# Linear branch in blocks of four tiles, and a transpose of two-token words, in a gated mix of softmax and linear attention

## The chip, the cores and the metric

One core of a Trainium2 chip runs the whole kernel. The metric is the time of one execution in device microseconds; lower is better. The kernel before is given by three runs, and one further execution was taken with the hardware profiler; the profile shows what every engine did in that execution.

## The reference, cut to what matters

The input x has 2048 tokens of 512 features in bf16. Two attention branches of 32 heads with 16 features per head read the same x, and a gate per token mixes their outputs.

```python
x = A_x                                               # (1, 2048, 512) bf16
g = _sigmoid((x * gate_w).sum(-1, keepdims=True))
# branch A: softmax attention, 32 heads of 16
scores = jnp.einsum("bhqd,bhkd->bhqk", q, k) * (Dh ** -0.5)
a = jnp.einsum("bhqk,bhkd->bhqd", _softmax(scores), v)      # then reshaped, @ wo
# branch B: linear attention with learned feature maps
pq = jnp.einsum("bhsd,hdf->bhsf", q, w_phi);  pk likewise from k
phi_q = jnp.concatenate([_softmax(pq), _softmax(-pq)], axis=-1);  phi_k likewise
kv = jnp.einsum("bhsf,bhsd->bhfd", phi_k, v);  z = jnp.einsum("bhsf->bhf", phi_k)
o = (phi_q @ kv) / (phi_q @ z + 1e-6)                       # then reshaped, @ wo
return g * a + (1 - g) * b
```

## The kernel before, in words

The kernel first describes all its work as a list of operations with their data dependences, a priority (`prio`, a due time counted in packs, below) and a modelled cost. `Plan.order` then writes one fixed queue per engine: at each step it takes the operation that can start first by its own costs, and among those that are ready the one with the lowest priority value. The queues are emitted as they stand, with semaphore waits. On the chip each engine works through its queue strictly in order. So every change of a cost, a due time or a share in the code can move instructions on all queues.

**Branch A, the attention.** Queries are cut into 4 chunks of 512, keys into 16 tiles of 128. A *unit* is one head, one key tile and one query chunk: scores of 128 keys by 512 queries in one PSUM bank. Four units, of four heads, make a *pack*; there are 512 packs and 2048 units. A group of 16 packs (all key tiles for four heads) accumulates into one bank. For each unit TensorE computes the scores (L979), somebody computes the exponential, and TensorE multiplies the result by the values (L1099). Two engines compute exponentials:

- ScalarE (ACT) takes the units called *mine*, in groups of three and two banks by turns (`GROUPS = (3, 2)`), one instruction a group (L1030). The five banks form a ring: the scores of group k wait for the exponential of group k-2.
- VectorE (DVE) takes the units called *away*. `SHARES` has one number for each of the 32 groups: how many of its 64 units go to DVE. A batch is mostly five units (`NB = 5`; `FIRST` and `LAST` give the sizes of the first and last batches). For each unit the scores are copied as scaled integers into `vt` (L880); then five instructions over the whole batch compute the exponential through `vf` into `vu` (L902, L904, L905, L906, L890). `vt` has two halves, `vf` one, `vu` three slots. The linear branch uses the same `vt` and `vf` as work space.

`_norm` follows every group of 16 packs. `n_t1` (L1128) transposes the accumulated bank in blocks of 32x32 into `T1` in f32, so that tokens lie on partitions. After every second group, `n_den` (L1135), `n_rec` (L1137) and `n_mul` (L1139) divide by the sum of the exponentials and the gate, with the result in `T2` in bf16, and `n_back` (L1144) transposes `T2` back into `onTA`. The last two of the 32 groups are normalised one by one (`alone`), the last one in four blocks of 128 tokens. `_out_a` (L1455) and `_out_last` (L1483) multiply `onTA` by the output weights, with 128 tokens of `onTA` as the stationary operand that TensorE loads.

**Branch B, the linear attention.** It works on token tiles of 128, two at a time: `_b_pair` projects two tiles (L682, evacuated at L1241 into `bq`), computes the softmax feature maps with a chain of 22 (keys) or 23 (queries) DVE instructions in `_b_exp`, `_b_scale` and the tail of `_b_pair` (L1258 to L1324), and uses `btree` for the maxima and sums. There are 8 pairs for the keys and 8 for the queries. `_b_kv` accumulates keys times values for four tiles; `_b_phit` transposes the query features by DMA and `_b_num` forms numerator and denominator. `K0, SK, Q0, SQ` space the due times of these pieces.

**Queue of SyncE (SP).** It issues the loads and all DMA transposes. At the start the order is: loads of x, the weights of branch B's keys (`wb1`) and others; the DMA transposes of x for the token blocks 2 and 3 (`xT<-xn`, L605); two loads of attention weights; then the DMA transpose of branch B's key weights (`WT<-WB`, L1200), which `_b_fuse` multiplies by the feature weights (L1209) and copies back with DVE (L1214). `KREL` is the pack from which the planner may issue that transpose, `XREL` the one from which the remaining attention weights may be loaded, `VREL0` the one for the first value projection, `OREL` the release of the last output products.

Of the kernel before, what the change touches and what calls it, by code (L numbers as in the profile page):

```python
# [7 lines left out]
ALU = mybir.AluOpType  # L8
AX = mybir.AxisListType

P = 128
D = 512
H = 32
DH = 16
TOK = 128
QCH = 512
SCALE = float(DH) ** -0.5
F32, BF16 = dt.float32, dt.bfloat16
# [4 lines left out]
EVEN, ODD = 0.34370964, 0.07826797  # L23
# [344 lines left out]
class _Kernel:  # L368
# [8 lines left out]
    XREL, KD, VD = 4, 8, 1  # L377
    BYDMA = (2, 3)
    KREL = 7
    EARLY = 27  # L380
    VREL0 = 3
    FIRST = (3, 4)
    LAST = (4, 3)
    OREL = 2
# [30 lines left out]
    def _memory(self, ctx):  # L415
# [50 lines left out]
        self.bq = sb("bq", [P, 3, 2, 2 * D], BF16)  # L466
        self.btree = sb("btree", [P, 32, 8, 4], BF16)
        self.bsum = sb("bsum", [P, P], F32)
        self.brec = sb("brec", [P, P], FP16)
# [319 lines left out]
    def _gate(self):  # L789
# [32 lines left out]
        for j in range(4):  # L822
# [6 lines left out]
    SHARES = (0, 3, 0, 12, 0, 4, 0, 13, 10, 4, 8, 2, 12, 3, 5, 8,  # L829
              5, 10, 13, 13, 0, 7, 6, 3, 12, 10, 12, 5, 11, 8, 13, 9)  # L830
# [290 lines left out]
    def _norm(self, ch, b0, nb, side, last, dst, b_dst, due, job, alone=False):  # L1121

        op = self.plan.op
        b1 = b0 + nb
        T1, T2, rinv = self.T1[:, :, b0:b1], self.T2[:, b0:b1], self.rinv[:, :, b0:b1]
        b_T1, b_T2, b_rinv = self.b_T1, self.b_T2, self.b_rinv
        part = nb / 16
        op("DVE", lambda e: e.transpose(T1[:, side].rearrange("p b s -> p (b s)"), self._bank(job)[:, 0:32 * nb]),  # L1128
           0.09 + 0.542 * part, deps=last, writes=[b_T1[side]], name="n_t1", prio=due - self.TPRIO, release=job)
        if not (side or alone):  # L1130
            return
        lo, hi = (side, side + 1) if alone else (0, 2)
        n, reads = hi - lo, b_T1[lo:hi]
        den, h = T1[:, lo:hi, :, 16], self.gh[:, 0, ch, b0:b1][:, None, :].to_broadcast([P, n, nb])
        op("DVE", lambda e: e.tensor_tensor(rinv[:, lo:hi], den, h, ALU.mult), 0.09 + 0.014 * n, reads=reads + [self.b_g],  # L1135
           writes=[b_rinv], name="n_den", prio=due)
        op("DVE", lambda e: e.reciprocal(rinv[:, lo:hi], rinv[:, lo:hi]), 0.063 + 0.1 * n * part, reads=[b_rinv],  # L1137
           writes=[b_rinv], name="n_rec", prio=due)
        op("DVE", lambda e: e.tensor_tensor(  # L1139
            T2.rearrange("p b (s d) -> p s b d", s=2)[:, lo:hi], T1[:, lo:hi, :, 0:16],  # L1140
            rinv[:, lo:hi, :, None].to_broadcast([P, n, nb, 16]), ALU.mult), 0.08 + 0.258 * n * part,
           reads=reads + [b_rinv], writes=[b_T2], name="n_mul", prio=due)
        if side == 1:
            op("DVE", lambda e: e.transpose(dst[:, 32 * b0:32 * b1], T2.rearrange("p b s -> p (b s)")), 0.09 + 0.537 * part,  # L1144
               reads=[b_T2], writes=[b_dst], name="n_back", prio=due)

    K0, SK, Q0, SQ = 18.0, 8.25, 191.0, 15.25

    def _branch_b(self):
        op, NT, NQC = self.plan.op, self.NT, self.NQC  # L1150
        B = Buf
        self.b_bq = [B() for _ in range(3)]
        self.b_WT = B()
        self.b_WP = [B() for _ in range(2)]
        self.b_tree, self.b_bsum, self.b_brec = B(), B(), B()
# [7 lines left out]
        self.outs, self.held = [], []  # L1163
        self.n_pair = 0
# [6 lines left out]
        for t in range(0, NT, 2):  # L1171
            due = self.K0 + self.SK * t
            self.linear.append((due, lambda t=t, due=due: self._b_keys(t, due)))
        for t in range(0, NT, 2):
            due = self.Q0 + self.SQ * t
            self.linear.append((due, lambda t=t, due=due: self._b_queries(t, due)))

    def _b_keys(self, t, due):
        self._b_v(t, due)
        self._b_v(t + 1, due + 1)  # L1180
        slots = self.held + [self._b_pair(1, t, due)]
        if t % 4 == 0:
            self.held = slots
            return
        self.held = []
        self._b_kv(t - 2, slots, due + 12)
        if t == self.NT - 2:
            self._b_kvbd(self.Q0 - 2)

    def _b_queries(self, t, due):  # L1190
        phi = self._b_pair(0, t, due)
        self._b_phit(t, phi, due + 12)
        self._b_num(t, due + 20)
        if t % 4 == 2:
            for tt in range(4):
                self._b_out(tt)
# [31 lines left out]
    def _b_pair(self, s, t0, due):  # L1228
        op = self.plan.op
        slot = self.n_pair % 3  # L1230
        self.n_pair += 1
        b = self.b_bq[slot]
        bq = self.bq[:, slot]
        war, parts = list(b.readers), []
        for k in range(2):
# [10 lines left out]
        b.writers, b.readers = parts, []  # L1246
        x = bq.rearrange("p t (g f i) -> p (t g) f i", f=DH, i=4)
        tree = self.btree[:]
        half = self.btree[:].bitcast(FP16)
        last = lambda t: t.rearrange("p (g i) -> p g i", i=4)  # L1250
        two = lambda n: 0.057 + n * 0.000525
        spread = lambda t: t[:, :, None, :].to_broadcast([P, 32, DH, 4])

        def chain(ops, off, bufs):
            for name, cost, fn in ops:
                op("DVE", fn, cost, reads=bufs, writes=bufs, name=name, prio=due + off)
        self._b_exp(bq, spread(tree[:, :, 0]), b, due, two)
        chain([("b_sum", two(1024), lambda e: e.tensor_tensor(half, x[:, :, 0:8], x[:, :, 8:16], ALU.add))]  # L1258
              + [("b_sum", two(128 * n), lambda e, n=n: e.tensor_tensor(half[:, :, 0:n], half[:, :, 0:n],
                                                                       half[:, :, n:2 * n], ALU.add)) for n in (4, 2)]  # L1260
# [284 lines left out]
```

## Time and profile before

| | |
|---|---|
| median of 3 runs | 841.67 us (841.08 to 842.1) |
| the profiled execution | 841.6 us |
| its span, first to last instruction | 839.8 us |
| granted TensorE clock | 1.000 |
| busy: PE, DVE, ACT | 803.1, 805.9, 828.9 us |
| instructions: PE, DVE, ACT | 8734, 1119, 736 |

The span is 1.8 us shorter than the time of the same execution; that rest lies outside the first and the last instruction. Busy times count an engine as busy while at least one of its instructions is under way, so successive instructions that overlap are counted once. Part of PE's work is filler: L1108 multiplies by zeros (3076 instructions in the page), which adds nothing to the result.

### The profile page before, as it was taken

Reading aid. Unit: us, or ns where it says so; the run is one execution under the profiler, and the core shown is the slowest. Engines: PE = TensorE matmul, PEld = TensorE weight load, DVE = VectorE, ACT = ScalarE, POOL = GpSimd, SP = SyncE. Lnnn points to the kernel's source line nnn. Section 1 sums busy time; section 2 is a strip of 40 time slices with the busy share of each in tenths; the row PEclk is TensorE's granted clock in tenths of the full one; section 3 lists DMA queues with packets and bytes.
Section 4 is the critical chain, followed back from the end, with each engine's and each line's share of the span. In section 5 each row is a group of like instructions: output and inputs, shape, how many; then the busy total and the mean of one; then the engine's idle time right before and its main releaser. Section 6 shows DMA issues by size and latency. Waiting matters only on the chain.

```text
span 839.8 us, 19654 instructions
## 1 busy us (share of the span) xinstructions
PE 803.1 (96%) x8734; PEld 265.0 (32%) x8776; DVE 805.9 (96%) x1119; ACT 828.9 (99%) x736; POOL 7.9 (1%) x14
## 2 busy tenths in 40 slices
PE   9999999999999999999999999999999999999997
PEld 5323333333322232223323233223322322322334
DVE  4799999999999999999999999999999999999995
ACT  7999999999999999999999999999999999999997
POOL 3000000000000000000000000000000000000000
PEclk9999999999999999999999999999999999999999
DMA  9700000000000000011101101102101100100000
GB/s 216 193 2 7 2 2 7 2 7 2 8 1 2 8 2 7 2 24 23 28 18 27 32 15 27 20 13 51 33 14 33 26 21 2 39 7 2 2 2 27
DMA packets 49028, 20.02 MB, mean 24 GB/s; under 512 B 38704, under 2 KB 48944, under 8 KB 48944
## 3 DMA queue, kind: packets, MB, share of 16 engines
q1 hardware_dynamic: 48272, 18.58, 9.9%
q8 instruction: 68, 1.11, 0.6%
q10 hardware_dynamic: 672, 0.20, 0.1%
q14 instruction: 16, 0.13, 0.1%
HBM read 6.31 MB, written 2.10 MB: 10 GB/s over the span
## 4 chain that ended last, share of the span: by engine, by line
ACT 74%; DVE 22%; PE 3%; issue 0%
ACT ET L1030 74%; DVE vt L880 3%; DVE vu L890 2%; DVE vf L902 1%; DVE vu L906 1%; DVE vf L905 1%; DVE bq L1306 1%; DVE VB L1225 1%; DVE vt L1298 1%; PE ps L979 1%; DVE bq L1308 1%; DVE bq L1241 1%; DVE bq L1318 1%; DVE vu L904 1%; DVE btree L1294 1%; DVE V L784 1%
## 5 line engine op out<-in xcount | busy, mean ns | idle before, releaser
L1030 ACT ACTIVATE ET<-ps 128x1536 bf16<-128x1536 f32 x731 | 826.6, 1375 | 0.8 <-PE ps L979 0.7
L979 PE MATMUL ps<-qT,kT 32*128 32x512 bf16 (+2 forms) x2248 | 320.6, 364 | 26.2 <-ACT ET L1030 17.0
L1108 PE MATMUL ps<-kT,zero 128*32 128x512 bf16 (+1 forms) x3076 | 256.9, 384 | 0.3 <-DVE rinv L1137 0.3
L1099 PE MATMUL ps<-ET,V 128*32 128x512 bf16 (+2 forms) x2000 | 195.8, 364 | 0.6 <-ACT ET L1030 0.3
L979 PEld LDWEIGHTS ps<-qT,kT 32*128 32x128 bf16 x2248 | 84.3, 91 | 304.1 <-ACT ET L1030 213.3
L880 DVE TENSOR_SCALAR vt<-ps 128x512 uint32<-128x512 f32 x221 | 145.6, 684 | 4.0 <-PE ps L979 3.8
L890 DVE SCALAR_TENSOR_TENSOR vu<-vt,vu 128x2560 int16<-128x2560 uint32 (+3 forms) x46 | 124.7, 2710 | 0.2
L1108 PEld LDWEIGHTS ps<-kT,zero 128*32 128x32 bf16 x3076 | 68.2, 95 | 107.2 <-issue 82.0
L1099 PE MATMUL ps<-vu,V 128*32 128x512 bf16 (+1 forms) x248 | 80.9, 359 | 0.0
L1099 PEld LDWEIGHTS ps<-ET,V 128*32 128x32 bf16 x2000 | 54.5, 96 | 56.4 <-issue 32.0
L905 DVE TENSOR_TENSOR vf<-vf 128x2560 f16<-128x2560 f16 (+3 forms) x46 | 65.8, 1430 | 0.3
L906 DVE TENSOR_TENSOR vu<-vu,vf 128x2560 f16<-128x2560 f16 (+3 forms) x46 | 65.8, 1429 | 0.3
L902 DVE TENSOR_SCALAR vf<-vt 128x2560 f16<-128x2560 uint8 (+3 forms) x46 | 65.9, 1432 | 0.2
L682 PE MATMUL ps<-WB,xT 128*128 128x512 bf16 x166 | 48.3, 382 | 3.1 <-issue 1.8
L904 DVE TENSOR_SCALAR vu<-vf 128x2560 f16<-128x2560 f16 (+3 forms) x46 | 36.4, 792 | 0.3
L682 PE MATMUL ps<-xT,WA 128*128 128x512 bf16 (+1 forms) x124 | 35.6, 379 | 0.1
L1128 DVE STREAM_TRANSPOSE T<-ps 128x512 f32<-128x512 f32 (+1 forms) x35 | 23.2, 662 | 4.7 <-PE ps L1099 4.7
L1099 PEld LDWEIGHTS ps<-vu,V 128*32 128x32 bf16 x248 | 21.6, 96 | 19.2 <-issue 13.1
L1241 DVE TENSOR_SCALAR bq<-ps 128x512 bf16<-128x512 f32 x32 | 21.7, 679 | 1.6 <-PE ps L682 1.6
L682 PEld LDWEIGHTS ps<-WB,xT 128*128 128x128 bf16 x192 | 14.4, 97 | 27.0 <-issue 12.2
L1306 DVE TENSOR_TENSOR bq<-vt 128x1024 f16<-128x1024 f16 x32 | 21.7, 678 | 0.3
L1298 DVE TENSOR_TENSOR vt<-vt,btree 128x2048 bf16<-128x2048 bf16 x16 | 19.5, 1218 | 0.3
(96 smaller groups left out, 442.5 us busy)
## 6 DMA issues: line engine op xcount, KB each, us to landing
qT<-qraw SPq DMA_DIRECT2D x120, 16.0 KB, 1.8
xn<-in_A_x_dram SPq DMA_DIRECT2D x3, 512.0 KB, 7.0
WB<-in_B_wqkv_dram SPq DMA_DIRECT2D x3, 512.0 KB, 6.9
out_dram<-WB SPq DMA_DIRECT2D x12, 128.0 KB, 1.7
WA<-in_A_wqkv_dram SPq DMA_DIRECT2D x3, 384.0 KB, 4.5
xn<-in_A_x_dram SPq DMA_DIRECT2D x2, 256.0 KB, 3.7
WoA<-in_A_wo_dram SPq DMA_DIRECT2D x1, 512.0 KB, 4.3
WoB<-in_B_wo_dram SPq DMA_DIRECT2D x1, 512.0 KB, 5.1
```

The costliest lines, as they stand in the source:

```text
L682: mm = op("PE", lambda e, c=c: e.matmul(self._bank(job)[:, 0:n], lhs(c), rhs(c), start=(c == 0), stop=(c == 3)), self.c_pe(n), reads=reads ...
L880: parts.append(op("DVE", lambda e, j=j, job=job: e.tensor_scalar(vt[:, j, :], self._bank(job), SCALE * LOG2E * 2.0 ** 24, 2.0 ** 31, op0=A ...
L890: o = op("DVE", lambda e: e.scalar_tensor_tensor(out=flat(vu).bitcast(I16), in0=flat(vt), scalar=2.0 ** -17, in1=flat(vu), op0=ALU.mult, o ...
L902: ("_frac", two, lambda e: e.tensor_scalar(vf, frac, 1 / 256, ROOT, op0=ALU.mult, op1=ALU.add), [b_vt], [b_vf]),
L904: lambda e: e.tensor_scalar(vu, vf, CUBE, SQUARE, op0=ALU.mult, op1=ALU.add), [b_vf], [b_vu]),
L905: ("_sq", two, lambda e: e.tensor_tensor(vf, vf, vf, ALU.mult), [b_vf], [b_vf]),
L906: ("_cube", two, lambda e: e.tensor_tensor(vu, vu, vf, ALU.mult), [b_vf, b_vu], [b_vu]),
L979: ins = e.matmul(out[u][:, cols], self.kT[32 * i:32 * i + 32, cp, kt * TOK:(kt + 1) * TOK], self.qT[32 * i:32 * i + 32, s, q], start=True, ...
L1030: o = plan.op("ACT", lambda e: e.activation(self.ET[:, a % NS:a % NS + n, :], self.ps[:, a % NR:a % NR + n, :], ACT.Exp, scale=SCALE), sel ...
L1099: ins = e.matmul(self._bank(ot)[32 * i:32 * i + 32, to], self.V[:, kt, g8 // 2, v0:v0 + 32], tile[:, cols], start=first and j == 0, stop=o ...
L1108: ins = e.matmul(self._bank(ot)[32 * i:32 * i + 32, lo:QCH], self.zero[:], self.kT[:, 0, lo:QCH], start=False, stop=False, tile_position=( ...
L1241: [lambda e, b, k=k: e.tensor_scalar(bq[:, k].rearrange("p (g s v) -> p g s v", g=8, s=2)[:, :, 0, :], b.rearrange("p (g v) -> p g v", g=8 ...
```

## The change

Two things change in the work, and the planner's constants change with them.

1. The linear branch works on four token tiles at a time where it can. `_b_part` replaces `_b_pair` and `_b_exp` and takes `nt` tiles: the keys' first eight tiles still go in four pairs (`PAIRS = 8`), the other eight in two blocks of four, and all queries in four blocks of four. The instructions are the same in kind, over twice as many elements in a block of four; `b_out` becomes two instructions, one for each sign. `btree` is gone: maxima and sums live in unused halves of `bq` and `vt`.
2. In `_norm`, for all but the last two groups, `n_t1` writes its transposed f32 values two words apart, so that the values of token q and token 256 + q stand side by side; `n_mul` writes them as adjacent bf16 values, and `n_back` transposes these as 256 words of 32 bits instead of 512 of 16 bits. `onTA` then holds two tokens interleaved, and `_tokens` reads every second element of it for the stationary operand of the output product.
3. `SHARES` and the other constants below are new: the number of units that DVE takes is 227 instead of 221.

```diff
-    XREL, KD, VD = 4, 8, 1
+    XREL, KD, VD = 13, 7, 6
-    KREL = 7
+    KREL = 3
-    VREL0 = 3
+    VREL0 = 1
-    LAST = (4, 3)
-    OREL = 2
+    LAST = (2,)
+    OREL = 1
...
-        self.bq = sb("bq", [P, 3, 2, 2 * D], BF16)
-        self.btree = sb("btree", [P, 32, 8, 4], BF16)
+        self.bq = sb("bq", [P, 2, 4, 2 * D], BF16)
...
-    SHARES = (0, 3, 0, 12, 0, 4, 0, 13, 10, 4, 8, 2, 12, 3, 5, 8,
-              5, 10, 13, 13, 0, 7, 6, 3, 12, 10, 12, 5, 11, 8, 13, 9)
+    SHARES = (0, 3, 0, 10, 1, 4, 0, 12, 8, 3, 11, 1, 10, 4, 14, 3,
+              4, 10, 11, 6, 10, 5, 8, 2, 14, 10, 12, 14, 4, 13, 14, 6)
...
     def _norm(self, ch, b0, nb, side, last, dst, b_dst, due, job, alone=False):
...
+            T1 = self.T1[:].rearrange("p a b d -> p (a b d)")
+            T2 = self.T2[:].rearrange("p b d -> p (b d)").rearrange("p (g d e) -> p g d e", g=16, e=2)
+            words = T1.rearrange("p (g d e) -> p g d e", g=16, e=2)
+            to = T1.rearrange("p (b s d e) -> p s e b d", b=8, s=2, e=2)[:, side]
+            rinv = self.rinv[:].rearrange("p s b -> p (s b)")
+            spread = rinv.rearrange("p (g e) -> p g e", e=2)[:, :, None, :].to_broadcast([P, 16, DH, 2])
...
+    def _normed(self, side, last, dst, b_dst, due, job, alone, to, T2, den, values, h, rinv, spread, n, reads, flat, part):
...
+        def gathered(e):
+            acc = self._bank(job)[:, 0:int(512 * part)]
+            return e.transpose(to, acc if alone else acc.rearrange("p (e b d) -> p e b d", e=2, b=8))
+        op("DVE", gathered, 0.09 + 0.542 * part, deps=last, writes=b_T1[side:], name="n_t1", prio=due - self.TPRIO, release=job)
...
-            op("DVE", lambda e: e.transpose(dst[:, 32 * b0:32 * b1], T2.rearrange("p b s -> p (b s)")), 0.09 + 0.537 * part,
+            word = (lambda t: t) if alone else (lambda t: t.bitcast(I32U))
+            op("DVE", lambda e: e.transpose(word(dst), word(flat)), 0.09 + (0.537 if alone else 0.27) * part,
                reads=[b_T2], writes=[b_dst], name="n_back", prio=due)
 
-    K0, SK, Q0, SQ = 18.0, 8.25, 191.0, 15.25
+    K0, SK, Q0, SQ = 16.0, 9.0, 186.0, 11.75
+    PAIRS = 8
...
+            if t < self.PAIRS or t % 4 == 0:
+                due = self.K0 + self.SK * t
+                self.linear.append((due, lambda t=t, due=due: self._b_keys(t, 2 if t < self.PAIRS else 4, due)))
+        for t in range(0, NT, 4):
             due = self.Q0 + self.SQ * t
             self.linear.append((due, lambda t=t, due=due: self._b_queries(t, due)))
...
-    def _b_pair(self, s, t0, due):
+    def _b_part(self, s, t0, nt, slot, due):
...
+        k, n, h, ng = self.n_bits % 2, 2 * nt * QCH, nt * QCH, 16 * nt
+        grid = self.vt[:, k, 0:nt].rearrange("p n q -> p (n q)").bitcast(BF16)
+        sums = grid.bitcast(FP16)[:, 0:h].rearrange("p (g f i) -> p g f i", f=8, i=4)
+        rest = self.vf[:, 0:nt].rearrange("p n q -> p (n q)").rearrange("p (a v) -> p a v", v=64)
+        even, odd = signs(flat.bitcast(FP16))[:, :, 0], signs(flat.bitcast(FP16))[:, :, 1]
+        tree = signs(flat)[:, :, 1].rearrange("p a (s u) -> p a s u", s=2)
...
+    def _tokens(self, qc, pr, tt):
+
+        on = self.onTA[:, qc % 3, pr]
+        if qc == self.NQC - 1 and pr == 3:
+            return on[:, tt * TOK:tt * TOK + TOK]
+        return on.rearrange("p (a q e) -> p e a q", a=2, e=2)[:, tt // 2, tt % 2]
+
     def _out_a(self, qc, tt, job, m, prs, due, stop=3, acquire=None):
...
-                return e.matmul(self._bank(job), self.onTA[:, qc % 3, pr, tt * TOK:tt * TOK + TOK],
+                return e.matmul(self._bank(job), self._tokens(qc, pr, tt),
```

## The prediction

> **What bounds the kernel now.** I first read the busy times (page, part 1): ACT 828.9 of 839.8 us, DVE 805.9, PE 803.1. Three engines at 96 to 99% do not yet say which one sets the time, so the next view is the busy time by stretch. Columns: length; PE, PEld, DVE, ACT and POOL busy with instruction counts; clock; DMA share; GB/s.
>
> ```profile
> 0.00:40.00 40.00, 37.89 (x355) 17.24 (x357) 23.10 (x41) 33.81 (x32) 7.92 (x14) 1.00 0.87 215
> 40.00:800.00 760.00, 731.33 (x7691) 230.04 (x7724) 752.42 (x1028) 759.79 (x674) 0.00 (x0) 1.00 0.07 14
> 800.00:840.00 40.00, 33.91 (x694) 17.73 (x695) 30.35 (x52) 35.28 (x33) 0.00 (x0) 0.99 0.05 15
> ```
>
> From 40 to 800 us ACT lacks 0.2 us and DVE 7.6 us of being busy throughout: both are full. Outside, DVE idles 16.9 us at the start and 9.7 us at the end. The waits say that ACT is the one that is fed in time:
>
> ```profile
> PEld ps L979 <- ACT ET L1030: 213.3, 487, 1.1
> ...
> ACT ET L1030 <- PE ps L979: 0.7, 2, 0.5
> ```
>
> Score loads wait for ACT 487 times, the exponentials for scores twice, 0.7 us in all. The timeline gives both ends of ACT's stream, and the last batch of DVE (columns: start, length, instruction):
>
> ```profile
> 7.94 8.45 ACT L1030 ACTIVATE ET<-ps 128x1536 bf16<-128x1536 f32 x7 [0.50 <-PE ps L979]
> ...
> 819.26 15.64 ACT L1030 ACTIVATE ET<-ps 128x1024 bf16<-128x1024 f32 x14
> ...
> 822.79 1.76 DVE L890 SCALAR_TENSOR_TENSOR vu<-vt,vu 128x1536 int16<-128x1536 uint32 x1
> ...
> 828.07 0.23 PE L1099 MATMUL ps<-vu,V 128*32 128x128 bf16 x1
> ```
>
> So the span is 7.94 us of start, 826.96 us of exponentials (7.94 to 834.90) and 4.9 us of tail. The time is ACT's stream, as long as DVE's queue, which is full too, delivers what PE's in-order queue waits for. The last batch is ready at 824.55 and first used at 828.07, 3.5 us later.
>
> **Durations.** Groups by form (count | busy us, mean ns):
>
> ```profile
> L1030 ACT ACTIVATE ET<-ps 128x1536 bf16<-128x1536 f32 x365 | 579.4, 1587 | 0.7 <-PE ps L979 0.7
> L1030 ACT ACTIVATE ET<-ps 128x1024 bf16<-128x1024 f32 x366 | 425.4, 1163 | 0.1
> ...
> L880 DVE TENSOR_SCALAR vt<-ps 128x512 uint32<-128x512 f32 x221 | 145.6, 684 | 4.0 <-PE ps L979 3.8
> L890 DVE SCALAR_TENSOR_TENSOR vu<-vt,vu 128x2560 int16<-128x2560 uint32 x41 | 115.4, 2814 | 0.2
> ...
> L1128 DVE STREAM_TRANSPOSE T<-ps 128x512 f32<-128x512 f32 x31 | 21.9, 708 | 0.0
> ...
> L1298 DVE TENSOR_TENSOR vt<-vt,btree 128x2048 bf16<-128x2048 bf16 x16 | 19.5, 1218 | 0.3
> ...
> L1304 DVE TENSOR_TENSOR vt<-vt,vf 128x1024 f16<-128x1024 f16 x16 | 10.9, 684 | 0.2
> ...
> L1144 DVE STREAM_TRANSPOSE onTA<-T 128x512 bf16<-128x512 bf16 x15 | 10.6, 706 | 0.0
> ...
> L1214 DVE CAST WB<-ps 128x512 bf16<-128x512 f32 x8 | 5.3, 685 | 0.0
> ...
> L1135 DVE TENSOR_TENSOR rinv<-T,gh 128x32 f32<-128x32 f32 x15 | 3.1, 204 | 0.0
> ...
> L1128 DVE STREAM_TRANSPOSE T<-ps 128x128 f32<-128x128 f32 x4 | 1.2, 304 | 4.7 <-PE ps L1099 4.7
> ```
>
> Neighbours overlap, so a mean is longer than its step. For DVE: three L880 at 330.09 take 1.88 us, a step of 0.60 against a mean of 0.684; I take 0.085 off every DVE mean.
>
> **ACT: six units fewer.** The new shares sum to 227 instead of 221. Built queues: 364 exponentials of three units, 364 of two and one of a single unit, against 365 and 366. A unit is worth 1.587 - 1.163 = 0.424. With 365 (b + 0.424) + 366 b = 826.96, a pair steps b = 0.920, a triple 1.344, a single 0.496. Removed: 1.344 + 2 x 0.920 - 0.496 = 2.69 us. All of it lies on the path, if nothing else is late.
>
> **DVE: the same total.** (a) Six more units: six L880, 6 x 0.60 = 3.6. Batches: 43 of five units against 41, one of four against two. The five instructions of a batch of five (2.814, 1.484, 0.817, 1.483, 1.482, less 5 x 0.085) step 7.66; those of four (2.288, 1.226, 0.684, 1.204, 1.202) 6.18. So 15.3 - 6.2 = 9.1, and 12.7 in all. (b) `n_back` on 256 words of 32 bits is not in the trace; bounds are the rows of 128 words (0.304) and of 512 16-bit elements (0.706). Transposes of 32-bit words cost 0.304 at 128 and 0.708 at 512, so 256 cost 0.439: 15 x 0.267 = 4.0 saved (0 to 6.0 by the bounds). (c) The linear chain has 16 x 22.5 = 360 instructions before and 6 x 23 + 4 x 24 = 234 after, over the same elements. An instruction's fixed part: 2048 elements cost 1.218, 1024 cost 0.684, so 0.150, less 0.085 overlap, about 0.07. 126 x 0.07 = 8.8 saved. Sum: 12.7 - 4.0 - 8.8 = -0.1 us.
>
> (d) `n_t1` now writes single f32 words two words apart, 30 times. No row shows such a write. Nearest are L1214, which reads PSUM in steps of 16 words at 0.685, like plain copies (0.684 to 0.689), and L1135, which reads single SBUF words 32 apart: 204 ns for 32 against 167 ns for 16 (its one call), 2.3 ns an element where transposes pay 1.05 (404 ns for 384). Bounds: nothing, and 1.26 ns x 512 = 0.65 us a call, 19 us in all; a gain is excluded, since as many words are moved. I take nothing, because L1214 has the same element count and L1135's difference of 37 ns is near the grain of such small instructions. [...]
>
> **Is there room for it?** ACT's stream shortens by 2.7 us while DVE's work stays, so DVE must idle less. The new DVE queue puts three of the L1214 copies (0.60 each) ahead of the third kT copy, in the stretch 13 to 27 us where DVE waits for PE by 0.5 to 1.6 us at a time: 1.8 us. And 126 fewer instructions in chains, where a reader of the previous result starts later (L905 at 344.19 after L904 at 343.32: 0.87 against a step of 0.75); if one in ten loses 0.12, 1.5 us. That makes 3.3, about what is needed. I keep 0.3 us of stall.
>
> **Moved steps with one answer.** SP's queue puts the WT transpose ahead of both xT transposes (before: 11.88 us for those, 18.69 for WT). It waits for `wb1`, then occupies SP for 2.8 to 3.8 us (5.57 for two xT, 3.84 for WT), so xT comes perhaps 1 us later; before, its first reader on PE ran at 18.03, 1.3 us after landing (11.88 + 4.8). PE's queue now waits for WT after the scores of 23 units (before: 48) and for xT after 28 (before: 25). Cover is about one exponential (1.3 us); beyond it, ACT stalls us for us. The three attention weights move behind both WT transposes and WoA, WoB; their readers come 73, 78 and 137 units in, later than before for the first two (40 and 58). The output product loads 63 of its 68 stationary tiles with a step of two elements: contiguous 98 ns; even doubled, 6 us among PE's 256.9 us of filler (L1108). LAST and OREL touch the tail; the chain after the last exponential is the same, 4.9 us, taken as unchanged within 0.5.
>
> **Sum.** 839.8 - 2.69 + 0.3 = 837.4 us of span; with the 1.8 us outside it, 839.2 us for an execution like the profiled one (841.6, against a median of 841.67, so no correction). Forecast 839.2 us, 0.3% faster.
>
> **Rivals.** *The stepped transpose costs.* For: L1135, and that DVE is full from 40 to 800 us, so each us there reaches PE's queue and then ACT. Against: L1214. Half the upper bound, 0.33 us x 30 = 10 us; less about 2 us of slack, 839.2 + 8 = 847 us (858 at the upper bound). [...] It decides from about 0.1 us a call: 3 us use up the slack and cancel the gain. Chance 0.16. *Late deliveries eat the gain.* A block of four holds one half of `vt`, and `vf`, for some 20 us of DVE work instead of 10; or the start stalls on the WT transpose. For: DVE lacked only 7.6 us in 760. Against: 0.7 us of ACT waits before. Stalls of 1 to 3 us: 840.0 to 842.0, centre 841. Chance 0.17. *DVE finds more room* and the tail shortens with the smaller last batch: 837.8. Chance 0.05. That the shares are not what runs is excluded by the built queues. The forecast's own case has the remaining 0.62.
>
> **Numbers.** A measurement can tell about 0.2% (1.7 us) from no change. Faster: the forecast's case, the better one, and 0.01 of the late deliveries: 0.68. Same, 840.0 to 843.3: most of the late deliveries and a little of the stepped transpose, 0.14. Slower: the rest, 0.18. The range runs from 838.0 to 844.5: it leaves out most of the stepped transpose (0.14) and part of the better case (0.04).
>
> **What would show it.** Right: L1030 runs 729 times, its stream takes 824 to 825 us, ACT waits for PE below 1.5 us in all, `n_t1` 128x512 stays at 0.71 us, `n_back` falls to 0.44 us, DVE idles less before 40 us. Wrong: `n_t1` above 0.8 us, and waits of ACT for scores whose releaser is DVE; or gaps of ACT between 14 and 25 us; or a linear block whose instructions cost more than twice those of a pair.

## The result, and the profile after

The changed kernel took 843.38 us (median of 15 runs, 841.65 to 845.69), the kernel before beside it 841.27 us (15 runs, 840.95 to 842.2). The ratio is 1.0025, with a 95% interval of 1.0018 to 1.0032: 2.1 us slower, where 2.5 us faster was forecast. The profiled execution of the changed kernel took 841.65 us with a span of 839.9 us at a clock of 1.000. It is the shortest of the 15, so two losses have to be found: 2.5 us of span against the forecast 837.4, made up of parts that a second profile of this kernel (`again`, below) shows as well, and 1.7 us more in the median, which this execution does not have.

Busy times by stretch, changed kernel (columns as before):

```profile
0.00:40.00 40.00, 38.57 (x381) 17.66 (x382) 27.13 (x50) 34.29 (x32) 7.92 (x14) 1.00 0.88 212
40.00:800.00 760.00, 727.95 (x7695) 230.47 (x7732) 747.62 (x907) 757.99 (x672) 0.00 (x0) 1.00 0.07 14
800.00:840.00 40.00, 33.75 (x706) 18.42 (x708) 29.29 (x49) 34.50 (x32) 0.00 (x0) 1.00 0.05 16
```

DVE found its room at the start (12.9 us idle before 40 us, where it was 16.9), as forecast. But between 40 and 800 us ACT now lacks 2.0 us where it lacked 0.2, and DVE lacks 12.4 us where it lacked 7.6. Over this stretch DVE is less full than before, so a lack of DVE time in sum is not what cost ACT its time.

Groups by form, changed kernel (count | busy us, mean ns | idle before, and its releaser):

```profile
L1029 ACT ACTIVATE ET<-ps 128x1536 bf16<-128x1536 f32 x364 | 580.0, 1594 | 2.5 <-PE ps L1098 1.8 <-PE ps L978 0.5
L1029 ACT ACTIVATE ET<-ps 128x1024 bf16<-128x1024 f32 x364 | 425.4, 1169 | 0.2 <-PE ps L978 0.2
...
L1151 DVE STREAM_TRANSPOSE T<-ps 128x512 f32<-128x512 f32 x31 | 22.0, 711 | 0.6 <-PE ps L1098 0.6
L1163 DVE STREAM_TRANSPOSE onTA<-T 128x256 uint32<-128x256 uint32 x15 | 6.5, 436 | 0.0
...
L1473 PEld LDWEIGHTS ps<-WoA,onTA 128*128 128x128 bf16 x48 | 3.8, 98 | 6.1 <-issue 4.1
```

The new prices that the rows show came out as forecast: `n_t1` (L1151) with its step of two words takes 711 ns against 708, `n_back` (L1163) 436 ns against an estimate of 439, and the strided stationary tile (L1473) loads in 98 ns, where the contiguous one took 97. The first row holds the news: ACT waited once for 1.8 us, for a product with the values (L1098).

The timeline of ACT's stream and, around its second row's end, DVE and PE (start, length, instruction; idle before it in brackets):

```profile
9.03 53.10 ACT L1029 ACTIVATE ET<-ps 128x1024 bf16<-128x1024 f32 x47 [0.21 <-PE ps L978]
62.09 129.28 ACT L1029 ACTIVATE ET<-ps 128x1536 bf16<-128x1536 f32 x114
193.16 640.95 ACT L1029 ACTIVATE ET<-ps 128x1536 bf16<-128x1536 f32 x567 [1.79 <-PE ps L1098]
```

```profile
181.96 0.84 PE L777 MATMUL ps<-WA,xT 128*128 128x128 bf16 x12
...
187.22 1.05 PE L1107 MATMUL ps<-kT,zero 128*32 128x512 bf16 x16
188.03 1.22 DVE L1310 TENSOR_TENSOR bq<-vt,bq 128x2048 uint16<-128x2048 bf16 x1
...
189.53 1.18 DVE L1312 TENSOR_TENSOR vt<-bq 128x2048 f16<-128x2048 bf16 x1
190.64 0.68 DVE L783 CAST V<-ps 128x512 bf16<-128x512 f32 x1
...
191.75 1.04 PE L681 MATMUL ps<-xT,WA 128*128 128x512 bf16 x4
192.71 1.05 PE L1098 MATMUL ps<-ET,V 128*32 128x512 bf16 x16
193.16 1.45 ACT L1029 ACTIVATE ET<-ps 128x1536 bf16<-128x1536 f32 x1 [1.79 <-PE ps L1098]
```

The value projection (L777) was done at 182.8, its copy into `V` (L783) came at 190.64, behind a normalisation and instructions of a linear block of four (L1310, L1312 among them), which carry an earlier due time. DVE is busy without a break in between, and all 1004 of its instructions stand in this profile in the order in which the built queue has them. Meanwhile PE multiplies zeros (L1107) and takes no exponentials from 185.83 to 192.71; the buffer of exponentials (`ET`) fills up and ACT stops, until the product with the values (L1098) frees a place. PE itself does not stand idle for the copy: its queue is fixed, and 1.4 us pass between the end of the copy (191.32) and the product, because zeros, scores and four other products (L681) stand ahead of it. This is the 14th of the 16 copies into `V`; in the kernel before, the 14th was done at 162.9.

The last lines of DVE in the changed kernel:

```profile
833.76 0.32 DVE L1151 STREAM_TRANSPOSE T<-ps 128x128 f32<-128x128 f32 x1 [6.32 <-PE ps L1098]
...
835.01 0.28 DVE L1151 STREAM_TRANSPOSE T<-ps 128x128 f32<-128x128 f32 x1
...
835.52 0.18 DVE L1157 RECIPROCAL rinv<-rinv 128x4 f32<-128x4 f32 x1
835.61 0.67 DVE L1511 CAST xT<-ps 128x512 bf16<-128x512 f32 x1
836.20 0.21 DVE L1159 TENSOR_TENSOR T<-T,rinv 128x64 bf16<-128x64 f32 x1
```

PE's queue has the last batch's products for the third token block at its very end (833.34, though the batch was ready at 825.17). So the third block is normalised at 833.76, directly ahead of the fourth (835.01), and an output copy (L1511) has slipped into the fourth's chain. Each of the two costs about 0.4 us: the fourth block's products ended at 834.58, and its reciprocal (L1157) at 835.70. The tail after the last exponential (834.11) is 5.8 us where it was 4.9.

### The profile page after: what moved, and what is told of

The parts are those of the page before. It is cut to its first block, busy times and chain, and to the rows that moved or that the text cites. A ratio compares the mean times of both kernels' runs of the same rounds, so it can differ in the third digit from the quotient of the medians.

```text
span 839.9 us, 19631 instructions
## 1 busy us (share of the span) xinstructions
PE 800.3 (95%) x8777; PEld 266.6 (32%) x8820; DVE 804.0 (96%) x1004; ACT 826.8 (98%) x734; POOL 7.9 (1%) x14
## 4 chain that ended last, share of the span: by engine, by line
ACT 96%; PE 3%; DVE 1%; issue 0%
ACT ET L1029 96%; PE ps L978 1%; PE ps L1107 1%; PE ps L633 0%; PE ps L1098 0%; PE ps L715 0%; DVE xT L1511 0%; PE ps L652 0%; PE ps L681 0%; PE ps L731 0%; DVE onTA L1163 0%; PE ps L1419 0%; PE ps L1348 0%; PE ps L1393 0%; DVE T L1151 0%
## 5 line engine op out<-in xcount | busy, mean ns | idle before, releaser
L1029 ACT ACTIVATE ET<-ps 128x1536 bf16<-128x1536 f32 x729 | 824.5, 1380 | 2.7 <-PE ps L1098 1.8
L978 PE MATMUL ps<-qT,kT 32*128 32x512 bf16 (+2 forms) x2248 | 317.1, 364 | 27.0 <-ACT ET L1029 19.5
L1107 PE MATMUL ps<-kT,zero 128*32 128x512 bf16 (+1 forms) x3120 | 256.8, 383 | 0.0
L1098 PE MATMUL ps<-ET,V 128*32 128x512 bf16 (+2 forms) x2003 | 194.0, 363 | 0.9 <-DVE vt L879 0.4
L879 DVE TENSOR_SCALAR vt<-ps 128x512 uint32<-128x512 f32 x227 | 147.6, 679 | 5.3 <-PE ps L978 4.7
L889 DVE SCALAR_TENSOR_TENSOR vu<-vt,vu 128x2560 int16<-128x2560 uint32 (+3 forms) x47 | 127.9, 2721 | 0.5
L1107 PEld LDWEIGHTS ps<-kT,zero 128*32 128x32 bf16 x3120 | 69.8, 95 | 104.0 <-issue 77.7
L1098 PE MATMUL ps<-vu,V 128*32 128x512 bf16 (+1 forms) x245 | 82.1, 367 | 0.0
L1098 PEld LDWEIGHTS ps<-ET,V 128*32 128x32 bf16 x2003 | 55.2, 96 | 60.2 <-issue 33.8
L904 DVE TENSOR_TENSOR vf<-vf 128x2560 f16<-128x2560 f16 (+3 forms) x47 | 67.5, 1436 | 0.4
L681 PE MATMUL ps<-WB,xT 128*128 128x512 bf16 x164 | 48.5, 382 | 3.9 <-issue 2.9
L681 PE MATMUL ps<-xT,WA 128*128 128x512 bf16 (+1 forms) x124 | 36.0, 380 | 0.1
L1151 DVE STREAM_TRANSPOSE T<-ps 128x512 f32<-128x512 f32 (+1 forms) x35 | 23.2, 664 | 6.9 <-PE ps L1098 6.9
L1098 PEld LDWEIGHTS ps<-vu,V 128*32 128x32 bf16 x245 | 21.7, 96 | 17.7 <-issue 13.1
L681 PEld LDWEIGHTS ps<-WB,xT 128*128 128x128 bf16 x192 | 14.2, 97 | 26.0 <-issue 14.2
L777 PE MATMUL ps<-WA,xT 128*128 128x128 bf16 x256 | 19.4, 220 | 0.0
L1300 DVE TENSOR_TENSOR vt<-vt,brec 128x4096 bf16<-128x4096 bf16 (+1 forms) x10 | 18.6, 1856 | 0.1
```

Of the source, the lines that this page charges most:

```text
L681: mm = op("PE", lambda e, c=c: e.matmul(self._bank(job)[:, 0:n], lhs(c), rhs(c), start=(c == 0), stop=(c == 3)), self.c_pe(n), reads=reads ...
L879: parts.append(op("DVE", lambda e, j=j, job=job: e.tensor_scalar(vt[:, j, :], self._bank(job), SCALE * LOG2E * 2.0 ** 24, 2.0 ** 31, op0=A ...
L889: o = op("DVE", lambda e: e.scalar_tensor_tensor(out=flat(vu).bitcast(I16), in0=flat(vt), scalar=2.0 ** -17, in1=flat(vu), op0=ALU.mult, o ...
L904: ("_sq", two, lambda e: e.tensor_tensor(vf, vf, vf, ALU.mult), [b_vf], [b_vf]),
L978: ins = e.matmul(out[u][:, cols], self.kT[32 * i:32 * i + 32, cp, kt * TOK:(kt + 1) * TOK], self.qT[32 * i:32 * i + 32, s, q], start=True, ...
L1029: o = plan.op("ACT", lambda e: e.activation(self.ET[:, a % NS:a % NS + n, :], self.ps[:, a % NR:a % NR + n, :], ACT.Exp, scale=SCALE), sel ...
```

## The experiments

The starting theory: ACT's saving is real and the code's prices are as costed; the time went into what waits in the queues. Its rival: the new forms (blocks of four, words) are dearer than their rows show. Ratios are against the kernel before, run beside each kernel (its medians 841.2 to 841.5).

**The changed kernel again (`again`).** No edit; where does the spread of the runs come from?

> The changed kernel as it is, for its spread. Theory T1 (TensorE loses single windows of its clock, and each costs about 1.2 us of ACT's stream): the runs fall between 841.7 and 845.7 us, and the time of a run rises with every 0.002 that its mean granted clock lacks of 1.000 (about +1.2 us each); runs of the kernel before stay at 840.9 to 842.2 with a clock of 1.000. Rival T2 (DVE's queue is late by chance in some runs): times vary at equal clock.

Measured: 843.33 us (9 runs), ratio 1.0025 (1.0015 to 1.0035). With the 15 runs above, sorted by granted clock, the mean times are 842.05 us at 1.000 (3 runs), 843.11 at 0.998 (12), 844.19 at 0.996 (6) and 845.23 at 0.994 (3): 1.07 us for each 0.002. The kernel before had 0.999 to 1.000 in each of its 39 runs in the first two sets of experiments. This profile (span 841.5) caught one such loss:

```profile
711.90:715.30 3.40, 3.38 (x39) 0.86 (x37) 3.37 (x5) 3.40 (x4) 0.00 (x0) 1.00 0.00 0
715.30:718.70 3.40, 2.50 (x21) 0.75 (x24) 3.40 (x6) 3.40 (x5) 0.00 (x0) 0.96 0.00 0
718.70:722.10 3.40, 3.40 (x27) 0.66 (x20) 3.37 (x3) 2.53 (x3) 0.00 (x0) 0.54 0.00 0
```

In the second stretch PE is busy for only 2.50 us, with 21 matmuls. In the third its clock (third column from the end) is 0.54, and ACT is busy for 2.53 of 3.40 us. In slices of 2 us the clock is 0.61 from 718 and 0.54 from 720, and 1.00 in the slices before and after: together 1.7 us of full clock lost. The lowest slices of `no_words` (from 518 and 548 us) and `v_fill` (from 762) have 0.50; at that clock 1.7 us are lost in 3.4 us. Of a span of 841.5 us, 1.7 us are 0.002, so a loss of 0.002 in the mean clock is one such stretch: the profiles of `no_words` and `words223`, both at 0.996, have two each, and that of `v_fill`, at 0.998, has one. So the median execution has lost one, about 1.1 of the 1.7 us; by the same count the slowest (0.994) have lost three. At equal clock the runs still differ by up to 1.0 us (841.65 to 842.63 at 1.000), and that part stays unexplained.

**The V copy (`v_early`).** The value projections are due eight packs earlier.

```diff
-        due = 32 * cp + 4 * j - (0.5 if cp else self.VD)
+        due = 32 * cp + 4 * j - (8.5 if cp else self.VD)
...
-                    rel=due - 20 if cp else -99 if j else self.VREL0, acquire=job if tt == 0 else None)
+                    rel=due - 12 if cp else -99 if j else self.VREL0, acquire=job if tt == 0 else None)
```

> The changed kernel with the value projections of the later head groups due 8 packs earlier (due 32*cp + 4*j - 8.5 instead of - 0.5). Theory T3 (ACT's one gap of 1.79 us at 191 to 193 us comes from the value copy that waits behind a block of four in DVE's queue): the gap is gone, the profiled span falls by 1.5 to 1.8 us against a run of the changed kernel at the same clock. Rival (the gap has another cause, such as DVE's work in all): a gap of the same size remains or comes elsewhere, and the time is the same within 0.5 us.

Measured: 842.12 us, ratio 1.0011 (1.0002 to 1.0021). The gap of 1.79 us is gone, with the 14th copy into `V` now at 172.52, which supports its cause. But the span did not fall by 1.5 to 1.8 us: it is 839.8 against 839.9. ACT's stream ends only 0.2 us earlier (833.91): four new gaps of 0.15 to 0.48 us have come, at 276, 367, 448 and 544 us. The due time had moved other things as well.

**Parts undone (`no_words`, `pairs16`, `old_consts`).** `no_words` takes back the two-token words and keeps every queue; `pairs16` does all keys in pairs; `old_consts` is the new code with all constants of before.

```diff
-            return e.transpose(to, acc if alone else acc.rearrange("p (e b d) -> p e b d", e=2, b=8))
+            return e.transpose(to, acc)
...
-            word = (lambda t: t) if alone else (lambda t: t.bitcast(I32U))
+            word = lambda t: t
```

> The changed kernel with the two-token words undone: n_t1 writes adjacent f32 words, n_back transposes 512 16-bit elements, the output product loads contiguous tokens; the planner's costs are left as they are, so that every queue keeps its order. DVE's work rises by 15 x 0.27 = 4.0 us. Theory T4 (DVE is full, so its work is on the path): 2 to 4 us slower than the changed kernel. Rival (PE and ACT set the time, DVE's queue has room): within 0.5 us of the changed kernel. If reading every second token cost PE time, this kernel would be faster.

Measured: 845.33 us, ratio 1.0044 (1.0029 to 1.0059): 843.35 us at clock 1.000, 844.94 and 845.72 at 0.998, 846.51 at 0.996. DVE's 4.0 us, put back into a queue planned without them, cost 1.3 us at the full clock (a single run) and 2.0 in the median. So with the order held fixed the amount of DVE's work does count, a third to a half of it.

```diff
-    PAIRS = 8
+    PAIRS = 16
```

> The changed kernel with all keys in pairs (PAIRS = 16; the queries stay in blocks of four); the queues are planned anew. DVE's work rises by 2 x 23 x 0.07 = 3.2 us. Theory T3 (a block of four with one due time holds back what is due in its midst): the gap at 191 to 193 us is gone or below 0.5 us, the time 0 to 1.5 us below the changed kernel's. Rival (DVE's total work counts): 2 to 3 us slower.

Measured: 854.1 us, ratio 1.0157 (1.0136 to 1.0178), clock 0.98 to 0.99, ACT waiting about 15 us. The forecast of the time was wrong. But the gap at 191 us is gone, as the theory had it:

```profile
61.92 307.00 ACT L1029 ACTIVATE ET<-ps 128x1536 bf16<-128x1536 f32 x271
```

The waits lie after 369 us, the longest (6.6 us) near the end. Whether the pairs' extra work or the new order made them was not separated.

```diff
-    XREL, KD, VD = 13, 7, 6
+    XREL, KD, VD = 4, 8, 1
...
-    LAST = (2,)
-    OREL = 1
+    LAST = (4, 3)
+    OREL = 2
...
-    K0, SK, Q0, SQ = 16.0, 9.0, 186.0, 11.75
+    K0, SK, Q0, SQ = 18.0, 8.25, 191.0, 15.25
```

(also `KREL`, `VREL0` and all of `SHARES`.)

> The changed kernel's code (blocks of four, two-token words) with all constants of the kernel before: DVE takes 221 units, and ACT the same 1827 as before; DVE has about 12.8 us less work than the changed kernel. Theory T5 (the new shares, which fill DVE and crowd TensorE in some groups, cause the gaps and the throttled windows): clock 0.999 to 1.000, no gap of ACT above 0.5 us, 841.0 to 842.0 us, as the kernel before. Rival T3b (the blocks of four cause them, whatever the shares): a gap of 1 us or more where a block of four of the keys ends, clock 0.998 or lower, 842.5 to 844 us.

Measured: 845.47 us, ratio 1.0051 (1.0034 to 1.0067), clock 1.000 in all 4 runs. Without the six units DVE is busy for only 794.2 us, the clock is whole, and the kernel is still 4.2 us slower than before: five ACT gaps of 0.24 to 0.58 us and a tail of 6.5 us. The theory had the clock right and the time wrong; the rival's gap of 1 us is not there. Yet a block of four holds back the 14th copy into `V` here too (188.51), and PE takes no exponentials for 6.7 us (183.98 to 190.64) where it took none for 6.9 us in the changed kernel, and ACT does not stop. So a late copy alone does not fix the cost; how full the buffer of exponentials is beforehand must count as well, which was not measured. Less work for DVE had not helped; this was the first sign that the amount alone was the wrong measure.

**Remedies that failed (`fill75`, `v_fill`, `v_tail`).** `fill75` raises the share of PE's time that the planner fills with products by zero; `v_fill` adds that to `v_early`; `v_tail` gives `v_early` the old batch sizes and release of the tail.

```diff
-    SPAN, SHARE, FILL = 2.7, 0.65, 0.2133
+    SPAN, SHARE, FILL = 2.7, 0.75, 0.2133
```

> The changed kernel with more filler on TensorE: the planner adds zero products while full-array work is below 0.75 of 2.7 us instead of 0.65 (3368 filler products against 3120). Theory T1 (single windows with little full-array work lose half the clock for 3.4 us, which costs ACT about 1.1 us each): the granted clock is 0.999 to 1.000 in most runs, and the median falls from 843.3 to about 842.0, the changed kernel's own time at full clock. Rival (the added filler delays scores by as much, or the clock drops for another reason): clock 0.998 and lower as before, time 843 us or more.

> Value projections due earlier (as in v_early) and the filler raised (as in fill75). If T1 and T3 are both right, they add: clock 0.999 or more and a median of 840.5 to 841.5 us, no ACT gap above 0.6 us. Rival (DVE's queue is too full for either to help): a median of 842 us or more at full clock.

Measured: `fill75` 844.84 us, ratio 1.0041 (1.0029 to 1.0053), `v_fill` 843.28, ratio 1.0023 (1.0014 to 1.0032); the clock is full in two of 6 and three of 10 runs. More filler did not keep the clock up, and they were 1.5 and 1.2 us slower than the same kernels without it.

```diff
-    LAST = (2,)
-    OREL = 1
+    LAST = (4, 3)
+    OREL = 2
```

> As v_early, with the tail's constants of the kernel before (LAST = (4, 3), OREL = 2). Theory T6 (the tail after the last exponential grew from 4.9 to 5.8 us because OREL = 1 and LAST = (2,) crowd TensorE's last products): the tail is 4.9 to 5.1 us, the time 0.6 to 0.9 us below v_early at equal clock. Rival (the tail's length comes from the order of the last units and outputs, which the six units moved): within 0.3 us of v_early.

Measured: 843.01 us, ratio 1.0024 (1.0015 to 1.0033). Its tail is 7.0 us where `v_early` has 5.9; the old values are worse here, and the theory of the tail was wrong.

**Slack for DVE (`u221`, `plan101`).** The theory had become: a DVE without slack lets PE wait for `vt`, and then the clock falls.

```diff
-    SHARES = (0, 3, 0, 10, 1, 4, 0, 12, 8, 3, 11, 1, 10, 4, 14, 3,
-              4, 10, 11, 6, 10, 5, 8, 2, 14, 10, 12, 14, 4, 13, 14, 6)
+    SHARES = (0, 3, 0, 10, 1, 4, 0, 12, 8, 3, 11, 1, 10, 4, 12, 3,
+              4, 10, 11, 6, 10, 5, 8, 2, 12, 10, 12, 12, 4, 13, 14, 6)
```

> The changed kernel's code and constants, but VectorE's shares of groups 14, 24 and 27 are 12 instead of 14: 221 units, so ACT has 2.4 to 2.7 us more and DVE 12.8 us less work. Theory (TensorE loses its full clock where its in-order queue waits for a DVE without slack): granted clock 0.999 or 1.000 in most executions, ACT stream 2 to 3 us longer than the changed kernel's, time 842 to 844.5 us, with a small spread between executions. Rival (the halved clock comes from the blocks of four or the words themselves, not from a full DVE): the clock stays at 0.996 to 0.998 and the time goes to 844.5 to 846.5.

Measured: 843.97 us, ratio 1.0034 (1.0021 to 1.0047), clock 0.999 or 1.000 in four of 5 runs. The gap of 1.79 us is unchanged; the tail is 4.9 us. This agreed with the theory as to the clock.

```diff
+        cost = 1.01 * cost if eng == "DVE" else cost
```

(in `Plan.op`, that is in the planner's numbers alone.)

> The changed kernel, but the planner's costs of DVE's work are 1 per cent higher, so that it writes queues in which DVE has a little slack; the work itself is the same 227 units. Theory (a full DVE whose queue is planned too tightly lets PE wait, and then the clock halves): waits of PE for vt become filler, clock 0.999 or more in more than half of the executions, 841 to 842.3 us. Rival (the amount of DVE work decides, not the plan): clock 0.996 to 0.998 as in the changed kernel and 843 to 844.5 us.

Measured: 860.25 us, ratio 1.0224 (1.0209 to 1.024), clock 0.98. The same work, ordered by costs 1% higher, takes 17 us more; the group line of ACT tells where the largest piece is.

```profile
L1030 ACT ACTIVATE ET<-ps 128x1536 bf16<-128x1536 f32 x364 | 573.4, 1575 | 16.6 <-PE ps L1099 10.5 <-PE ps L979 5.9
```

One wait of 10.5 us ends at 840.66, near the end. Neither forecast came: slack in the plan did not keep the clock, and with the amount of work unchanged the time did not stay. The order that comes out can cost far more than the six units are worth.

**The words alone (`before_words`, `words223`, `words_same`).** The kernel before with nothing but the words of two tokens; then with two more units for DVE; then with the words in exactly the queues of before. Of `words_same` against `before_words`:

```diff
-        op("DVE", gathered, 0.09 + 0.542 * part, deps=last, writes=b_T1[side:], name="n_t1", prio=due - self.TPRIO, release=job)
+        op("DVE", gathered, 0.09 + 0.542 * part, deps=last, writes=[b_T1[side]], name="n_t1", prio=due - self.TPRIO, release=job)
```

> The kernel before with the words of two tokens alone: n_t1 in steps of two words, n_back on 256 words, strided stationary operands; pairs, shares, constants and planner costs as before. Price theory: n_back 0.44 us in place of 0.71, so DVE busy 4.0 us less, n_t1 128x512 at 0.71; ACT still sets the end with the same 221 units, so the time is that of before within 0.5 us: 840.8 to 841.8. Rival (the words cost something that the groups do not show, in PE's loads or in waits): 842.5 us or more.

> The kernel before with the words of two tokens, their lower cost told to the planner, and two more units on DVE (223; groups 20 and 23 have one more each), so that DVE spends the 4.0 us that the words save. ACT work falls by 0.8 to 0.9 us. Theory (words are a real saving, and pairs keep the deliveries in time): 840.2 to 841.0 us at a clock of 0.999 or more, faster than both. Rival (any new order with a fuller DVE makes new waits of ACT or halved clock): 841.5 to 843.5.

> The kernel before with the words of two tokens, and every queue in exactly the order of before (in before_words a dependence of n_t1 had moved instructions, and the end of PE's queue with them). DVE has 4.0 us less work, nothing else differs. Price theory (the words cost nothing anywhere, and 4.0 us of DVE's time are worth nothing while ACT sets the end): 840.9 to 841.6 us, clock 0.999 or more, tail 4.9 us, ACT stream 826.7 to 827.1. Rival (the words themselves cost what before_words lost): 842.5 to 843.5, with the tail at 6 us or more.

Measured: `before_words` 843.33 us, ratio 1.0034 (1.0019 to 1.0048); `words223` 844.27, ratio 1.0037 (1.0024 to 1.0049), with a tail of 6.9 us, ACT gaps of up to 0.97 us and a clock of 0.994 to 1.000, which are the waits and the clock that its rival had named, and slower still; `words_same` 841.34, ratio 1.0001 (0.9991 to 1.001). In `words_same` the fourth transpose of the gate (L806, at 57.19 us) writes into words that the first `n_t1` (54.73 us) has filled, so the first pair of groups holds other numbers; every instruction, size and queue place is there. Its groups:

```profile
L1152 DVE STREAM_TRANSPOSE T<-ps 128x512 f32<-128x512 f32 x31 | 21.8, 704 | 0.0
L1164 DVE STREAM_TRANSPOSE onTA<-T 128x256 uint32<-128x256 uint32 x15 | 6.5, 436 | 0.0
```

In this kernel the words cost nothing and bring nothing by themselves: ACT sets the time. The single dependence by which `before_words` differs moves instructions, among them the products of the last token block. In the kernel before, 48 of the 64 run at 833.47 and only 16 follow the last exponential:

```profile
834.95 0.41 PE L1099 MATMUL ps<-ET,V 128*32 128x128 bf16 x16 [0.30 <-ACT ET L1030]
```

In `before_words` all come together, behind the output products, at 835.98 us, although the last exponential ended at 834.56:

```profile
835.98 1.08 PE L1099 MATMUL ps<-ET,V 128*32 128x128 bf16 x64
...
837.11 0.32 DVE L1152 STREAM_TRANSPOSE T<-ps 128x128 f32<-128x128 f32 x1 [1.75 <-PE ps L1099]
```

The tail is 6.9 us instead of 4.9, and 2.0 us is the whole difference between `before_words` and `words_same`, at the same clock of 1.000.

**Other orders of the changed kernel (`v_224`, `v_221`, `v_226`, `v_228`).** If the order lost the gain, another order of the same work must show it. `v_224` and `v_221` are `v_early` with 13 and 12 in place of 14 units in groups 14, 24 and 27. `v_226` and `v_228` are two orders chosen for their built queues, in which neither the 14th copy into `V` nor the last batch is held back: value projections ten packs earlier, and few units moved.

```diff
-        due = 32 * cp + 4 * j - (0.5 if cp else self.VD)
+        due = 32 * cp + 4 * j - (10.5 if cp else self.VD)
...
-                    rel=due - 20 if cp else -99 if j else self.VREL0, acquire=job if tt == 0 else None)
+                    rel=due - 12 if cp else -99 if j else self.VREL0, acquire=job if tt == 0 else None)
...
-              4, 10, 11, 6, 10, 5, 8, 2, 14, 10, 12, 14, 4, 13, 14, 6)
+              3, 10, 11, 6, 10, 5, 8, 2, 14, 10, 12, 14, 4, 13, 14, 6)
```

(`v_226`; the second half of `SHARES` in `v_228` is 3, 10, 11, 7, 10, 4, 8, 2, 14, 10, 12, 14, 5, 13, 14, 7.)

> The changed kernel with the value projections due 8 packs earlier (as in v_early) and the shares of groups 14, 24 and 27 at 13 instead of 14: 224 units, ACT 1.3 us more and DVE 6.4 us less work than the changed kernel. Theory (two named causes, the held V copy and a DVE without slack, cost the gain): clock 0.999 or more in most runs, no ACT gap of over 0.6 us, median 840.3 to 841.3, a little faster than before. Rival (every new order brings new small waits and its own tail): 841.5 to 843.

> As v_224, but those three shares are 12: 221 units as before the change. ACT work equals that of before, so the best that it can reach is before's time. Theory (with DVE slack nothing is lost): 841.0 to 842.0, clock 0.999 or more in nearly all runs. Rival: 842.5 or more from new small gaps and the tail, at the same clock.

> The changed kernel with the value projections due 10 packs earlier, so that the V copies stand ahead of the blocks of four in DVE's queue, and one unit less on DVE (group 16: 3 instead of 4). ACT work is 0.4 us more than in the changed kernel, 824.9 us from the rows. Theory (the gain was lost to the order of the queues, not to a price of the new code: the held V copy, the last batch of DVE, crowded groups): in the built queues DVE's last batch now stands ahead of the copies of the output, so the tail should be 4.9 us, and ACT's gaps 0.5 us or less: 7.4 + 824.9 + 0.5 + 4.9 + 1.8 = 839.5 at the full clock; with one half-clock window in some runs a median of 839.3 to 840.8, faster than both. Rival (blocks of four with a fuller DVE lose the gain in any order): 841.5 or more.

> As v_226, and shares moved by one unit in groups 19 (7), 21 (4), 28 (5) and 31 (7): 228 units, ACT work 824.1 us from the rows. Theory: gaps 0.5 us, tail 5.1 us: 838.9 at the full clock, median 838.7 to 840.3. Rival (one unit over what DVE can carry makes PE wait for vt and the clock halve): 841 or more, clock 0.998 or less in most runs.

Measured: `v_224` 850.2 us, ratio 1.0075 (1.0044 to 1.0106): three of its 5 runs at 850.2 to 850.4 with a clock of 0.988, two at 844.55 and 845.14 with 0.998 and 0.995; in the profiled one ACT waits at twelve places after its first exponential. `v_221` 843.39, ratio 1.003 (1.002 to 1.0039), clock 1.000 in seven of 10 runs. `v_221` came out as its rival had it and `v_224` worse: with slack for DVE and the gap at 191 us gone, both are still slower than the kernel before. `v_226` 839.33 us, ratio 0.998 (0.9971 to 0.9989), clock 0.999 or 1.000 in ten of 11 runs; `v_228` 838.48 us, ratio 0.9966 (0.9954 to 0.9979), clock 1.000 in all 5. Both are faster than the kernel before, which ran beside them, and than the changed kernel's 843.38. The 14th copy into `V` in `v_226`, the timeline of `v_226`, then of `v_228`, and the stretch 40 to 800 us of `v_228`:

```profile
163.71 0.69 DVE L783 CAST V<-ps 128x512 bf16<-128x512 f32 x1
```

```profile
7.52 54.67 ACT L1029 ACTIVATE ET<-ps 128x1536 bf16<-128x1536 f32 x48 [0.50 <-PE ps L978]
62.13 769.96 ACT L1029 ACTIVATE ET<-ps 128x1536 bf16<-128x1536 f32 x681
```

```profile
62.07 768.94 ACT L1029 ACTIVATE ET<-ps 128x1536 bf16<-128x1536 f32 x680
```

```profile
40.00:800.00 760.00, 727.92 (x7662) 229.94 (x7701) 750.12 (x908) 759.87 (x674) 0.00 (x0) 1.00 0.07 14
```

ACT has no gap any more after 62 us, while DVE is busy for 806.2 us in `v_228`, more than in the changed kernel (804.0), with the same 14 units in groups 14, 24 and 27. The last copy into `V` still stands behind a block of four in `v_226` (190.01), but ACT does not wait for it. `v_226`: 7.52 us of start, 824.57 of stream, 4.9 of tail. So the same code, with one unit less or more on DVE, brings the forecast gain in another order: the order had lost it, not a price of the new code.

## Why the prediction was wrong, point by point

- *ACT: six units fewer, 2.69 us.* Right. The stream is 826.74 us (7.37 to 834.11) and has 2.2 us of gaps in it, so 824.5 us of exponentials, against 824.3 forecast.
- *DVE: the same total.* Right in that no time was added (804.0 us busy against 805.9, a fall of 1.9 us where 0.1 was forecast) and in (b) and (d); (c) was not measured by itself. At (d) nothing was taken for the step of two words, and `n_t1` with it takes 711 ns where the dense one takes 708; the upper bound was 0.65 us more a call. The rival *the stepped transpose costs*, which took half of that bound, was wrong.
- *Moved steps with one answer.* The start was 0.6 us shorter (7.37 against 7.94), ACT did not wait for WT or xT, and the strided tiles load as fast (98 ns against 97). Wrong was the tail "taken as unchanged within 0.5": 5.8 us against 4.9. The chain is the same, as argued, but what stands ahead of it in PE's and DVE's queues is not. Going back to the old constants of the tail does not mend it: 7.0 us in `v_tail`.
- *"I keep 0.3 us of stall."* This step failed. It was 2.2 us, 1.79 of them in one wait. The step asked whether DVE has enough time in sum, and it had. It did not ask, for each copy that PE's products need, what stands ahead of it in DVE's queue, nor how late it comes. Of its own signs of being right, ACT's waits for PE below 1.5 us (they are 2.5) and a stream of 824 to 825 us failed, and none of its signs of being wrong describes this wait. The rival *late deliveries eat the gain* came nearest and had 0.17: it named late deliveries behind a block of four, though through the work space that the block holds (`vt`, `vf`), where the runs show its place in the queue ahead of the copy into `V`. Its 840 to 842 us hold two of the three executions at the full clock (841.65, 841.88; the third took 842.63).
- The rest was in no case: the clock of TensorE, 1.000 in the profile of before, was taken for granted. It fell in 21 of 24 runs and added about 1.3 us to the median (843.38 against a mean of 842.05 at the full clock), at 1.07 us for each 0.002. That 843.38 lies within the stated 838.0 to 844.5 is luck: the range was drawn for stalls and a little of the dearer transpose, and some 1.3 us of the time came from the clock, which it did not consider.

The sum again, for the profiled execution: 837.4 forecast − 0.6 (start) + 2.2 (stream 826.74 against 824.57) + 0.9 (tail) = 839.9, the span. With the order mended, the profiled execution of `v_226` spans 837.0 us and takes 839.07, and its median is 839.33, where 837.4 and 839.2 were forecast with one unit more on DVE. That its stream equals the forecast one to 0.01 us (824.57) is partly chance: it has 0.4 us more exponentials and less stall than was forecast.

Still open: what exactly makes the clock fall in one order and not in another. How long PE was busy just before does not tell it: the case shown follows a stretch with PE busy for 2.50 of 3.4 us (from 715.3), but `v_226` (2.42 of 3.4 us from 463.3) keeps a clock of 1.00 after such a stretch; and the 4 us from 758 in which the loss in `v_fill` begins have PE busy for 3.48, but `no_words` keeps 1.00 during and after 4 us with 3.07 (from 194). And why `v_224` is so much worse than `v_early` and `v_221`, between which it lies, was not followed up.

## What to carry to other kernels

Where an engine's queue is fixed, fusing many small steps into one long chain of nearly equal priority has two costs: its work, and what it holds back. Read, for each transfer that the bounding engine waits for, what stands ahead of it in the new queue, and read the last 10 us of each queue instruction by instruction; both were in the built queues before any run. And compare a change of code with its order held fixed before it is judged: here the order was worth from −4 us (`v_226`, which even has one unit more on ACT) to +17 us (`plan101`), more than the 2.5 us that the change itself was to bring.

## What the runs showed of the hardware

- One stretch of about 3.4 us at half of TensorE's clock costs 1.07 us in the changed kernel, which ScalarE bounds (24 runs at four clocks); the profile of `again` shows it as a granted clock of 0.54 in a single stretch of 3.40 us, the average over the run as 0.998. The price is not the same in every order: in `v_early` the five runs at 0.997 take 842.19 us on average, the three at 0.999 and 1.000 take 841.75.
- A 32x32 transpose on VectorE that writes f32 two words apart costs what a dense one does (711 ns over 31 calls in the changed kernel, of which 30 write so, and 704 to 712 in nine other profiles with this write; 708 dense, in the kernel before); on 256 words of 32 bits it takes 436 ns in the changed kernel, where 512 elements of 16 bits take 706 in the kernel before.
- Loading a stationary tile whose columns lie two elements apart takes 98 ns (48 loads in the changed kernel), where a contiguous one takes 97 (48 in the kernel before).
